# Attention scores on four quarters of the array, with v loaded by pairs of heads and rows of two weights permuted

## The chip, the cores and the metric

The kernel runs on one core of one Trainium2 chip. The metric is the device time of one execution in microseconds (us); the figure quoted for a kernel is the median of its runs. Engines are named as in the profile: PE is the matrix engine (PEld its weight loads), DVE the vector engine, ACT the scalar engine, POOL the GpSimd engine, SP the engine whose queue issues most of the DMAs ("SPq").

## The reference

The inputs q, k and v have 4 batches, 8 heads, 576 positions and 64 features per head. The positions are cut into 9 chunks of 64, and attention stays within a chunk. The result, laid out as 2304 tokens of 512 features, goes through a bilinear MLP and then through an MLP with a rational activation:

```python
scores = scale * np.matmul(q_c, k_c.transpose(0, 1, 2, 4, 3))
scores = scores - np.max(scores, axis=-1, keepdims=True)
attn = np.exp(scores)
attn = attn / (np.sum(attn, axis=-1, keepdims=True) + 1e-09)
x = np.matmul(attn, v_c)                  # then 2304 tokens x 512 features
x = ((x @ w_a) * (x @ w_b)) @ w_out       # 512 -> 1536 -> 512
...                                       # second MLP, 512 -> 2048 -> 512
```

A chunk's scores for one head are a product of 64x64 by 64x64, all in float32. Weights come as float64.

## The kernel before, in words

Activations are kept transposed: features on the 128 partitions, tokens along the free axis. The array has 128 rows (the contraction) and 128 columns (the output partitions); a product of 64 by 64 occupies one of its four quarters, given by a group of 64 rows and a group of 64 columns.

**Attention** works in 18 units of 128 tokens, which are two chunks c = 0, 1. `a_load` (line 270) brings q, k and v of a unit on SP, one DMA each of 256 KB with 128 partitions (chunk and position) by 8 heads by 64 features. A unit whose two chunks lie in different batches (units 4 and 13) takes two DMAs of 64 partitions each instead. `a_transpose` (294) turns k and q by PE into (h2, d) on the partitions, where a pair of heads hp holds heads 2 hp and 2 hp + 1 and h2 says which. `a_scores` (305) makes 16 products. Product (hp, c, h2) reads rows h2 of qT and kT and writes partitions h2 of one PSUM tile:

```python
r, cols = (slice(n * CH, (n + 1) * CH) for n in (h2, c))
nc.tensor.matmul(ps[r, 2 * hp + c, :], qT[r, hp, cols], kT[r, hp, cols], ...)
```

So the row group and the column group of a product are both h2, and two of the four quarters are used. A float32 product is two MATMUL instructions, so a unit has 32 of them at line 313. DVE then takes the maximum over the keys (317, one instruction of 128x512), subtracts it (319) and ACT takes the exponential (320). `a_soft` (323) normalizes, `a_ptrans` (331) transposes the probabilities by PE, and `a_pv` (342) multiplies with v: 16 products, row group c, column group h2, in the order (row, column) = (0,0), (0,1), (1,0), (1,1), with one PSUM tile for each c. ACT copies the two tiles out as the rounded part of x (358), DVE makes the low part (362). The transposes of units 4 and up, the scores of all, and the products with v of units 4 and up take their PSUM from `ps_at`, a pool of two buffers.

**Order of work.** The program is written out by hand in issue order for each engine. The four units of the first block of tokens come at the start in the order of the list FIRST (line 70: k and q transposes, S scores, E softmax, P transpose, V product with v, L low part, w one weight tile rounded, d products that nothing reads), their loads and the first four weight tiles in that of LOADS (73). Then come the loads of the two small operands ca and cb (545, 546), then, as tiles are rounded, more weight tiles, eight ahead, and after the last item of FIRST the loads of unit 4 (570). All of these DMAs are issued by SP, one after the other. The 14 later units are spread over the first MLP of the block of tokens before theirs: `a_pieces` (366) gives each piece a due time in twelfths of the unit's share, and `fill` (582) calls it between the halves of a step. There the pieces stand in PE's stream between long runs of products of the two MLPs. The load of v of the next unit is issued right behind the product with v (373), that of k and q behind the transpose of q.

**Weights.** `w_fetch` (137) loads one tile of 512 KB by one DMA. For w_a and w_b (and w_in of the second MLP) a tile is 128 columns of the matrix, with 128 partitions by 4 groups of rows by 1 KB (122). The 128 rows that share a group kk are contracted at once by `ab_half` (411). ACT and DVE round the tile (162 to 216) and w_out tiles come as 128 rows of 4 KB.

Of the kernel before, what the change touches and what calls it, by code (L numbers as in the profile page):

```python
# [20 lines left out]
def chunk_attention_two_mlps(  # L21
# [14 lines left out]
    """Chunked attention, a bilinear MLP, and an MLP with a rational activation.  # L36

    Activations are kept transposed (features on partitions, tokens along the free axis), so
    every product contracts over partitions without a transpose between layers. A float32
    operand x of the four large products is held as hi + lo, both float32r with 12 significant  # L40
    bits: hi is x rounded, lo = x - hi is exact. Then x @ w = hi @ w_hi + lo @ w_hi + hi @ w_lo
    in three passes of the tensor engine; lo @ w_lo lies below float32's rounding.

    The weights come as the bits of float64 (int64 of the same shape) and are rounded to float32
    here, from the two words H and L of an element. H, read as float32 and times 2**-112, has
    float32's exponent of the element in the bits 27 to 23 and the upper 20 bits of its fraction in
    the bits 22 to 3 of the word that three places further left are the element's without its sign
    and the last three bits; round(L * 2**-29) is added for those, and the sign is that of H in a
    float16 too small for any other bit. (An element below 2**-119 becomes one of that size or 0.)
    """  # L50
# [14 lines left out]
    # ln is taken of Q * 2**-LSH, which keeps it inside the table's range for any finite Q.  # L65
    LSH = 60
    # Order of the attention of the first block: transposes of k and q, scores, softmax, transpose of
    # its result, product with v and the low part of that; w: a weight tile is rounded; d: the tensor
    # engine is kept busy.
# [4 lines left out]
    # Tiles of weights that are loaded ahead of those rounded.  # L74
    AHEAD = 8
    # The attention of a block is spread over this part of the 3 * F1 places of the block before.
    SPAN = 33
    AN = 1280
    # Blocks of tokens of the first MLP. The first one is large: its steps wait for the weights.
# [3 lines left out]
    # Blocks of tokens of the second MLP.  # L83
# [27 lines left out]
    # ---------------------------------------------------------------- weights  # L111
# [5 lines left out]
    for nm, w, n, col in (("a", w_a, F1, True), ("b", w_b, F1, True), ("o", w_out, F1, False),  # L117
                          ("i2", w_in2, F2, True), ("o2", w_out2, F2, False)):
        bits = w.bitcast(I32)
        for i in range(n):  # L120
            if col:
                w_src[nm, i] = bits[:, 2 * i * P:2 * (i + 1) * P].rearrange("(k p) f -> p k f", p=P)
            else:
                w_src[nm, i] = bits[i * P:(i + 1) * P, :]
# [12 lines left out]
    def w_fetch():  # L137
        key = order[n_cv[0]]
        at = n_cv[0] + AHEAD
        n_cv[0] += 1  # L140
        if at < len(order1):
            t = p_w.tile([P, DM, 2], I32, name="w_raw", tag=f"w{at}")
        else:
            t = p_st.tile([P, DM, 2], I32, name="w_raw", tag="w_raw")
        dst = t.rearrange("p f t -> p (f t)")
        src = w_src[key]
        if len(src.shape) == 3:
            dst = dst.rearrange("p (k f) -> p k f", k=src.shape[1])
        nc.sync.dma_start(out=dst, in_=src)  # L149
        raws[key] = t  # L150
# [11 lines left out]
    def w_front(finish=lambda: None):  # L162
        """What ACT has to do with the next weight tile to be rounded, and the loads ahead of it."""
        while n_cv[0] < len(order) and n_cv[0] < n_cv[1] + (
            AHEAD if n_cv[0] + AHEAD < len(order1) else 3 if n_cv[0] < len(order1) else 2
        ):
            w_fetch()
        if n_cv[1] == len(order):
            held_w.append(finish)
            return  # L170
        t = raws.pop(order[n_cv[1]])
        hw = t[:, :, 1]
        lw = t.rearrange("p f t -> p (f t)").bitcast(U16).rearrange("p (f t) -> p f t", t=4)[:, :, 1]
        # Room for the terms: where the parts of the tile will be, or one more of p_st.
        if order[n_cv[1]] in w2_d:
            t = p_st.tile([P, 2, DM], I32, name="w_cz", tag="w_raw")
            c, z = t[:, 0], t[:, 1]
        else:
            c, z = w_tile(order[n_cv[1]], I32)
        zz = z.bitcast(F16).rearrange("p (f t) -> p f t", t=2)  # L180
        nc.scalar.activation(c.bitcast(F32), hw.bitcast(F32), AF.Copy, scale=2.0 ** -112)
        nc.scalar.activation(zz[:, :, 1], hw.bitcast(F32), AF.Copy, scale=2.0 ** -112)
        front_w.append((c, z))

        def rest():
            finish()
            nc.scalar.activation(zz[:, :, 0].bitcast(U16), lw, AF.Copy, scale=2.0 ** -13)

        held_w.append(rest)
# [5 lines left out]
    def w_next(n, hold=False):  # L195
        """Round the next n weight tiles; those of the first MLP stay on chip, those of the second
        go back to memory as float32. What is left of the last one comes with the next call."""
# [33 lines left out]
    def w2_next():  # L231
        """Split the next weight tile of the second MLP."""
# [16 lines left out]
    # -------------------------------------------------------------- attention  # L249
# [7 lines left out]
    # q, k and v of the units of the first block, where the last weights will be.  # L257
# [4 lines left out]
    # A ring of tokens for x and then for y.  # L262
# [7 lines left out]
    def a_load(u, *names):  # L270
        """[(c, s), h, d] for the chunks c = 0, 1 of unit u"""
        (b0, c0), (b1, c1) = divmod(2 * u, NCH), divmod(2 * u + 1, NCH)
        for nm, src in (("k", k), ("q", q), ("v", v)):
# [9 lines left out]
            if b0 == b1:  # L283
# [10 lines left out]
    def a_transpose(u, nm):  # L294
        """[(c, s), hp, (h2, d)] -> [(h2, d), hp, (c, s)]"""
# [9 lines left out]
    def a_scores(u):  # L305
        """[(h2, q), (hp, c), key], less its maximum over the keys; its exponential"""
        qT, kT = un.pop(("qT", u)), un.pop(("kT", u))
        ps = ps_at.tile([P, H, CH], F32, name="at", tag="at")
        for hp in range(HP):
            for c in range(2):  # L310
                for h2 in range(2):
                    r, cols = (slice(n * CH, (n + 1) * CH) for n in (h2, c))
                    nc.tensor.matmul(  # L313
                        ps[r, 2 * hp + c, :], qT[r, hp, cols], kT[r, hp, cols], start=True, stop=True
                    )
        m = p_e.tile([P, H], F32, name="m", tag="m")
        nc.vector.tensor_reduce(m, ps, AX.X, ALU.max)
        e = (p_t0 if u < U0 else p_t).tile([P, H, CH], F32, name="e", tag="T")
        nc.vector.tensor_tensor(e, ps, m.unsqueeze(2).to_broadcast([P, H, CH]), ALU.subtract)
        nc.scalar.activation(e, e, AF.Exp, scale=SCALE)  # L320
        un["e", u] = e
# [9 lines left out]
    def a_ptrans(u):  # L331
        """[(h2, q), hp, (c, key)] -> [(c, key), hp, (h2, q)]"""
# [9 lines left out]
    def a_pv(u):  # L342
        """x^T: [(h2, d), hp, (c, q)], a bank for each c: c is the row group of its products."""
        pT, vv = un.pop(("pT", u)), raw.pop(("v", u))
        ps = []
        for c in range(2):
            pool, tag = (ps_acc, "acc") if u < U0 else (ps_at, "at")
            ps.append(pool.tile([P, HP, CH], F32, name="at", tag=tag))
        for hp in range(HP):
            for c in range(2):  # L350
                for h2 in range(2):
                    r, cols = (slice(n * CH, (n + 1) * CH) for n in (c, h2))
                    nc.tensor.matmul(  # L353
                        ps[c][cols, hp, :], vv[r, 2 * hp + h2, :], pT[r, hp, cols], start=True, stop=True
                    )
        out = [[t[:, :, x_at(u * P + c * CH, CH)] for t in (x_hi, x_lo)] for c in range(2)]
        for c, (hi, lo) in enumerate(out):
            nc.scalar.copy(hi, ps[c])  # L358

        def low():  # L360
            for c, (hi, lo) in enumerate(out):
                nc.vector.tensor_tensor(lo, ps[c], hi.bitcast(F32), ALU.subtract)  # L362
# [3 lines left out]
    def a_pieces(u):  # L366
        """With the twelfth of the time at which each is due."""
# [8 lines left out]
    # -------------------------------------------------------- constants a, b  # L376
# [4 lines left out]
    # ---------------------------------------------------------------- phase 1  # L381
# [45 lines left out]
    # ---------------------------------------------------------------- phase 2  # L427
# [9 lines left out]
    def y_split(j, kk):  # L437
        """For even blocks where x was, for odd ones where the last weights of the first MLP were."""
# [19 lines left out]
    def g_front(j, i):  # L458
        """Denominator less 1 + 1e-6 and numerator less a0, both from h."""
# [13 lines left out]
    def g_back(u, t):  # L473
        """Their quotient: 1 / Q as exp(-ln Q) and one Newton step."""
# [59 lines left out]
    def warm(n):  # L534
        """Products that nothing reads: the tensor engine's clock falls while it idles."""
# [43 lines left out]
    for j in range(NB):  # L579
# [11 lines left out]
        for i in range(F1):  # L591
            def w_more(part):
                """At an even pace, three tiles ahead of those in use."""
# [82 lines left out]
```

## Time and profile before

| | |
|---|---|
| median of 3 runs | 939.78 us (937.49 to 939.79) |
| span of the profiled execution | 934.7 us |
| median less span (what lies around the span) | 5.1 us |
| PE busy | 917.6 us, 98% of the span |
| DVE, ACT busy | 613.2 us (66%), 588.4 us (63%) |
| DMA queue of SP | 91776 packets, 67.65 MB |

The span runs from the first to the last instruction of the profiled execution. Its own total time is not listed apart from the runs, so the difference to the median stands for what lies around the span. Busy time of PE is modelled from start times and lengths; where one matmul overlaps the next, the chain of waits tells better what a group costs. "Idle before" in a row is the time in which the engine stood still just before those instructions.

### The profile page before, as it was taken

What the parts mean: (1) busy time and instruction counts of PE and PEld (TensorE: products, weight loads), DVE (VectorE), ACT (ScalarE), POOL (GpSimd) and SP (SyncE); (2) the same over time, 40 slices, a digit from 0 to 9 for tenths busy, and PEclk for the clock granted to TensorE, in tenths of its full rate; (3) what the DMA queues carried; (4) which work ended last, traced back from release to release, by engine and by line L of the source; (5) the groups of instructions that cost most, each with busy time, mean ns of one, the idle gap of its engine ahead of it and who ended that gap; (6) DMA issues with size and microseconds to landing.
All of it is one profiled execution on the core that took longest, in us unless ns stands there. A gap on an engine that the chain in (4) does not pass through costs nothing.

```text
span 934.7 us, 14740 instructions
## 1 busy us (share of the span) xinstructions
PE 917.6 (98%) x5828; PEld 829.9 (89%) x5828; DVE 613.2 (66%) x1074; ACT 588.4 (63%) x1068; POOL 18.1 (2%) x38
## 2 busy tenths in 40 slices
PE   6799999999999999999999999999999999999998
PEld 6688889999999999999999999888888888888997
DVE  3787863334443344344255579999879988998886
ACT  5899983225445445444244488877677767767775
POOL 0000000000000000000000000000000000000000
PEclk8999999999999999999999999999999999999999
DMA  9983242214445453443154300020011002000100
GB/s 226 278 274 115 87 149 80 58 40 137 132 133 158 133 162 124 124 147 102 53 155 148 109 34 1 1 80 1 1 40 52 1 1 79 1 0 1 46 1 35
DMA packets 97863, 81.72 MB, mean 87 GB/s; under 512 B 59648, under 2 KB 83712, under 8 KB 97792
## 3 DMA queue, kind: packets, MB, share of 16 engines
q1 hardware_dynamic: 91776, 67.65, 25.2%
q0 software_dynamic: 2560, 8.39, 2.4%
q10 hardware_dynamic: 3456, 4.72, 1.4%
q8 instruction: 46, 0.75, 0.4%
q14 instruction: 25, 0.20, 0.1%
HBM read 62.92 MB, written 17.83 MB: 86 GB/s over the span
## 4 chain that ended last, share of the span: by engine, by line
PE 95%; SPq 3%; DMA 1%; issue 0%; ACT 0%
PE acc L242 13%; PE acc L243 12%; PE acc L244 12%; PE ab L242 11%; PE ab L244 11%; PE ab L243 11%; PE h L242 7%; PE h L244 7%; PE h L243 7%; PE at L313 2%; SPq L291 2%; PE at L300 1%; SPq L149 1%; DMA k<-in_k_dram 1%; PE at L353 1%; PE at L337 1%
## 5 line engine op out<-in xcount | busy, mean ns | idle before, releaser
L242 PE MATMUL ab<-x_hi,w 128*128 128x384 f32 (+2 forms) x576 | 196.8, 342 | 0.7 <-ACT x_hi L358 0.7
L243 PE MATMUL ab<-x_lo,w 128*128 128x384 f32 (+2 forms) x576 | 193.0, 335 | 0.0
L244 PE MATMUL ab<-x_hi,w 128*128 128x384 f32 (+2 forms) x576 | 193.0, 335 | 0.0
L242 PEld LDWEIGHTS ab<-x_hi,w 128*128 128x128 f32 x576 | 108.5, 188 | 5.8 <-ACT x_hi L358 0.9
L244 PE MATMUL acc<-w,g_lo 128*128 128x512 f32 x288 | 112.6, 391 | 0.0
L243 PE MATMUL acc<-w,g_hi 128*128 128x512 f32 x288 | 112.6, 391 | 0.0
L242 PE MATMUL acc<-w,g_hi 128*128 128x512 f32 x288 | 112.1, 389 | 0.0
L243 PEld LDWEIGHTS ab<-x_lo,w 128*128 128x128 f32 x576 | 108.6, 189 | 3.9 <-DVE x_lo L362 0.3
L244 PEld LDWEIGHTS ab<-x_hi,w 128*128 128x128 f32 x576 | 108.4, 188 | 3.8
L465 ACT ACTIVATE a_ring<-h 128x512 f32<-128x512 f32 (+1 forms) x80 | 44.2, 552 | 86.4 <-PE h L244 86.4
L242 PE MATMUL acc<-g_hi,w 128*128 128x384 f32 (+2 forms) x288 | 98.4, 342 | 0.0
L244 PE MATMUL acc<-g_hi,w 128*128 128x384 f32 (+2 forms) x288 | 96.4, 335 | 0.0
L243 PE MATMUL acc<-g_lo,w 128*128 128x384 f32 (+2 forms) x288 | 96.4, 335 | 0.0
L425 DVE TENSOR_TENSOR g_lo<-a_ring,g_hi 128x384 fp32r<-128x384 f32 (+2 forms) x72 | 40.1, 557 | 80.3 <-ACT g_hi L422 80.3
L419 DVE TENSOR_TENSOR a_ring<-ab,a_ring 128x384 f32<-128x384 f32 (+2 forms) x72 | 39.9, 554 | 78.0 <-PE ab L244 77.8
L608 ACT COPY a_ring<-ab 128x384 f32<-128x384 f32 (+2 forms) x72 | 34.4, 478 | 73.0 <-PE ab L244 72.5
L468 DVE SCALAR_TENSOR_TENSOR u<-u,cb_t,a_ring 128x512 f32<-128x512 f32 (+1 forms) x80 | 55.6, 696 | 28.8 <-ACT u L466 28.1
L244 PE MATMUL h<-x_hi,w 128*128 128x384 f32 (+1 forms) x192 | 68.0, 354 | 0.0
L242 PE MATMUL h<-x_hi,w 128*128 128x384 f32 (+1 forms) x192 | 68.0, 354 | 0.0
L243 PE MATMUL h<-x_lo,w 128*128 128x384 f32 (+1 forms) x192 | 67.9, 353 | 0.0
L244 PEld LDWEIGHTS acc<-w,g_lo 128*128 128x128 f32 x288 | 54.0, 188 | 11.3
L422 ACT CAST g_hi<-a_ring 128x384 fp32r<-128x384 f32 (+2 forms) x72 | 36.2, 503 | 43.7 <-DVE a_ring L419 43.7
(85 smaller groups left out, 1828.4 us busy)
## 6 DMA issues: line engine op xcount, KB each, us to landing
w_raw<-in_moe_w_out_dram SPq DMA_DIRECT2D x28, 512.0 KB, 4.7
w_raw<-in_moe_w_in_dram SPq DMA_DIRECT2D x16, 512.0 KB, 4.2
w_raw<-in_moe_w_a_dram SPq DMA_DIRECT2D x12, 512.0 KB, 6.6
w_raw<-in_moe_w_b_dram SPq DMA_DIRECT2D x12, 512.0 KB, 6.8
out_dram<-o SPq DMA_DIRECT2D x18, 256.0 KB, 2.5
w_i<-w_x POOLq DMA_DIRECT2D x16, 256.0 KB, 2.3
w_o<-w_x POOLq DMA_DIRECT2D x16, 256.0 KB, 2.3
w_raw<-w_i SPq DMA_DIRECT2D x16, 256.0 KB, 2.7
```

What stands on the lines that cost most here:

```text
L149: nc.sync.dma_start(out=dst, in_=src)
L242: nc.tensor.matmul(ps, wh, xh, start=first, stop=False)
L243: nc.tensor.matmul(ps, wh, xl, start=False, stop=False)
L244: nc.tensor.matmul(ps, wl, xh, start=False, stop=last)
L291: nc.sync.dma_start(out=dst, in_=s.rearrange("h s d -> s h d"))
L313: nc.tensor.matmul(ps[r, 2 * hp + c, :], qT[r, hp, cols], kT[r, hp, cols], start=True, stop=True)
L419: nc.vector.tensor_tensor(a_s, ps_b, a_s, ALU.mult)
L422: nc.scalar.copy(hi, a_s)
L425: return lambda: nc.vector.tensor_tensor(lo, a_s, hi.bitcast(F32), ALU.subtract)
L465: nc.scalar.activation(ah, ps, AF.Abs)
L468: nc.vector.scalar_tensor_tensor(u, u, cb_t[:, 0:1], ah, ALU.add, ALU.mult)
L608: nc.scalar.copy(a_s, ps_a)
```

## The change

Scores: the product (hp, c, h2) now writes the partitions of chunk c, into a PSUM tile of its own for each h2. Its row group is h2 and its column group is c, so all four quarters are used, in the order (row, column) = (0,0), (1,0), (0,1), (1,1). Maximum and subtraction are done for each of the two tiles (four DVE instructions of 128x256 in place of two of 128x512). The probabilities then lie with (chunk, query) on partitions, and their transpose has (h2, key) there. So v is loaded with h2 and key on the partitions: four DMAs for each unit, of 64 partitions by 4 heads. The product with v has h2 as its row group and b as its column group (head 4b + 2a + h2), in the same order of quarters as the scores. This leaves the features of x in another order, which the rows of w_a and w_b follow: a tile of theirs is loaded by two DMAs of 64 partitions each. Comments and docstrings are also blanked.

```diff
@@ weights
                 w_src[nm, i] = bits[:, 2 * i * P:2 * (i + 1) * P].rearrange("(k p) f -> p k f", p=P)
+                if nm in "ab":
+                    w_src[nm, i] = bits[:, 2 * i * P:2 * (i + 1) * P].rearrange(
+                        "(b k d) f -> b d k f", b=2, d=D
+                    )
@@ w_fetch
-        nc.sync.dma_start(out=dst, in_=src)
+        if len(src.shape) == 4:
+            for b in range(2):
+                nc.sync.dma_start(out=dst[b * D:(b + 1) * D], in_=src[b])
+        else:
+            nc.sync.dma_start(out=dst, in_=src)
@@ a_load
-            if b0 == b1:
+            if nm == "v":
+                t = t.rearrange("p (c a) d -> p c a d", c=2)
+                parts = [
+                    (t[h2 * CH:(h2 + 1) * CH, c], src[bb, h2::2, cc * CH:(cc + 1) * CH, :])
+                    for c, (bb, cc) in enumerate(((b0, c0), (b1, c1)))
+                    for h2 in range(2)
+                ]
+            elif b0 == b1:
@@ a_scores
-        ps = ps_at.tile([P, H, CH], F32, name="at", tag="at")
+        ps = [ps_at.tile([P, HP, CH], F32, name="at", tag="at") for _ in range(2)]
...
-                    nc.tensor.matmul(
-                        ps[r, 2 * hp + c, :], qT[r, hp, cols], kT[r, hp, cols], start=True, stop=True
-                    )
+                    nc.tensor.matmul(ps[h2][cols, hp, :], qT[r, hp, cols], kT[r, hp, cols], start=True, stop=True)
-        nc.vector.tensor_reduce(m, ps, AX.X, ALU.max)
-        nc.vector.tensor_tensor(e, ps, m.unsqueeze(2).to_broadcast([P, H, CH]), ALU.subtract)
+        for h2 in range(2):
+            nc.vector.tensor_reduce(m[:, h2], ps[h2], AX.X, ALU.max)
+        for h2 in range(2):
+            nc.vector.tensor_tensor(
+                e[:, :, h2], ps[h2], m[:, h2].unsqueeze(2).to_broadcast([P, HP, CH]), ALU.subtract
+            )
@@ a_pv
-            ps.append(pool.tile([P, HP, CH], F32, name="at", tag=tag))
+            ps.append(pool.tile([P, 2, P], F32, name="at", tag=tag))
...
-                    nc.tensor.matmul(
-                        ps[c][cols, hp, :], vv[r, 2 * hp + h2, :], pT[r, hp, cols], start=True, stop=True
-                    )
+                        nc.tensor.matmul(
+                            ps[h2][cols, a, q], vv[r, c, 2 * b + a, :], pT[r, 2 * b + a, q], start=True, stop=True
+                        )
```

In the new `a_pv` the loops run over a, c, b, h2, outermost first, with `r, cols, q` for h2, b, c. The copies of x out of PSUM and its low part stay two of 128x256 for each unit.

## Rows read from the trace of the kernel before

**Rows 1.** Span and busy time of the engines, from the page's head and part 1.

```profile
span 934.7 us, 14740 instructions
...
PE 917.6 (98%) x5828; PEld 829.9 (89%) x5828; DVE 613.2 (66%) x1074; ACT 588.4 (63%) x1068; POOL 18.1 (2%) x38
```

**Rows 2.** Windows, core 0: stretch and length in us, busy us per engine, PEclk, DMA share, GB/s.

```profile
50.00:60.00 10.00, 10.00 (x64) 8.30 (x61) 8.92 (x17) 10.00 (x18) 0.00 (x0) 1.00 1.07 367
...
140.00:450.00 310.00, 310.00 (x2594) 301.90 (x2592) 124.03 (x249) 137.23 (x269) 16.74 (x31) 1.00 0.39 118
```

**Rows 3.** Chain of waits in order of time: start us, us on the chain, what.

```profile
146.68 1.08 PE at L313 x32
...
147.76 0.32 PE ab L242
...
158.53 0.62 PE at L353 x32
...
159.16 0.32 PE ab L242
...
337.87 0.62 PE at L353 x32
...
433.12 1.08 PE at L313 x32
```

**Rows 4.** Line 353 on PE's queue: count, then min/median/max ns.

```profile
L353 PEldq EVENT_SEMAPHORE  x19: 51/51/318, 28.5 to 446.1; - x19
```

**Rows 5.** Instruction groups by line and shape: count, busy us, mean ns, idle before.

```profile
L362 DVE TENSOR_TENSOR x_lo<-at,x_hi 128x256 fp32r<-128x256 f32 x36 | 13.4, 417 | 11.6 <-ACT x_hi L358 11.5
...
L317 DVE TENSOR_REDUCE m<-at 128x8 f32<-128x512 f32 x18 | 12.4, 691 | 38.7 <-PE at L313 38.5
```

**Rows 6.** DMA issues on SP, lines 291 and 149: count, min/median/max ns.

```profile
L291 SPq DMA_DIRECT2D v<-in_v_dram x16: 367/368/2899, 35.8 to 423.8; - x16
...
L291 SPq DMA_DIRECT2D kqv<-in_k_dram x4: 432/1118/2517, 0.7 to 13.5; - x4
...
L149 SPq DMA_DIRECT2D w_raw<-in_moe_w_a_dram x12: 367/466/1465, 2.9 to 114.7; - x12
```

**Rows 7.** The same for line 291, 312 to 314 us only: two pieces of half height.

```profile
L291 SPq DMA_DIRECT2D v<-in_v_dram x2: 607/617/627, 312.2 to 312.9; - x2
```

**Rows 8.** Timeline of SP, first 31 us: start us, us, line, issue.

```profile
13.45 2.52 SPq L291 DMA_DIRECT2D kqv<-in_k_dram  x1
16.02 0.96 SPq L291 DMA_DIRECT2D kqv<-in_v_dram  x1
17.02 1.15 SPq L149 DMA_DIRECT2D w_raw<-in_moe_w_a_dram  x1
18.21 0.56 SPq L291 DMA_DIRECT2D kqv<-in_v_dram  x1
18.82 1.04 SPq L545 DMA_DIRECT2D ca_t<-in_moe_a_dram  x1
19.90 1.52 SPq L546 DMA_DIRECT2D cb_t<-in_moe_b_dram  x1
21.46 0.44 SPq L149 DMA_DIRECT2D w_raw<-in_moe_w_b_dram  x1
...
29.38 1.74 SPq L291 DMA_DIRECT2D k<-in_k_dram  x2
```

**Rows 9.** Windows of the opening: busy us per engine, PEclk, DMA share, GB/s.

```profile
23.00:24.00 1.00, 0.70 (x7) 0.46 (x5) 0.95 (x3) 0.78 (x2) 0.00 (x0) 1.00 0.76 51
24.00:25.00 1.00, 0.00 (x0) 0.00 (x0) 0.95 (x3) 0.87 (x3) 0.00 (x0) 1.00 0.46 84
```

**Rows 10.** Chain of waits around the first load of unit 4.

```profile
30.15 9.96 DMA k<-in_k_dram
40.24 0.63 PE at L300 x4
```

**Rows 11.** Waits: who for whom, us in total, times, longest.

```profile
PE at L300 <- DMA k<-in_k_dram: 1.1, 1, 1.1
```

More of the change, by code (lines that the diff above doesn't have):

```diff
@@ L146, in w_fetch @@
         src = w_src[key]
-        if len(src.shape) == 3:
-            dst = dst.rearrange("p (k f) -> p k f", k=src.shape[1])
-        nc.sync.dma_start(out=dst, in_=src)
+        if len(src.shape) > 2:
+            dst = dst.rearrange("p (k f) -> p k f", k=src.shape[-2])
+        if len(src.shape) == 4:
[3 more added lines that the diff above has]
+            nc.sync.dma_start(out=dst, in_=src)
         raws[key] = t
@@ L312, in a_scores @@
                     r, cols = (slice(n * CH, (n + 1) * CH) for n in (h2, c))
[L313 to L319 removed]
+                    nc.tensor.matmul(ps[h2][cols, hp, :], qT[r, hp, cols], kT[r, hp, cols], start=True, stop=True)
+        m = p_e.tile([P, 2, HP], F32, name="m", tag="m")
+        e = (p_t0 if u < U0 else p_t).tile([P, HP, 2, CH], F32, name="e", tag="T")
+        for h2 in range(2):
[4 more added lines that the diff above has]
+            )
         nc.scalar.activation(e, e, AF.Exp, scale=SCALE)
[L321 removed]
+        un["e", u] = e.rearrange("p a b d -> p (a b) d")
     def a_soft(u):
@@ L345, in a_pv @@
         ps = []
-        for c in range(2):
+        for h2 in range(2):
             pool, tag = (ps_acc, "acc") if u < U0 else (ps_at, "at")
-            ps.append(pool.tile([P, HP, CH], F32, name="at", tag=tag))
-        for hp in range(HP):
+            ps.append(pool.tile([P, 2, P], F32, name="at", tag=tag))
+        for a in range(2):
             for c in range(2):
-                for h2 in range(2):
-                    r, cols = (slice(n * CH, (n + 1) * CH) for n in (c, h2))
-                    nc.tensor.matmul(
-                        ps[c][cols, hp, :], vv[r, 2 * hp + h2, :], pT[r, hp, cols], start=True, stop=True
-                    )
-        out = [[t[:, :, x_at(u * P + c * CH, CH)] for t in (x_hi, x_lo)] for c in range(2)]
-        for c, (hi, lo) in enumerate(out):
-            nc.scalar.copy(hi, ps[c])
+                for b in range(2):
+                    for h2 in range(2):
+                        r, cols, q = (slice(n * CH, (n + 1) * CH) for n in (h2, b, c))
+                        nc.tensor.matmul(
+                            ps[h2][cols, a, q], vv[r, c, 2 * b + a, :], pT[r, 2 * b + a, q], start=True, stop=True
+                        )
+        out = [
+            [t.rearrange("p (a b) n -> p b a n", b=2)[:, h2, :, x_at(u * P, P)] for t in (x_hi, x_lo)]
+            for h2 in range(2)
+        ]
+        for h2, (hi, lo) in enumerate(out):
+            nc.scalar.copy(hi, ps[h2])
         def low():
-            for c, (hi, lo) in enumerate(out):
-                nc.vector.tensor_tensor(lo, ps[c], hi.bitcast(F32), ALU.subtract)
+            for h2, (hi, lo) in enumerate(out):
+                nc.vector.tensor_tensor(lo, ps[h2], hi.bitcast(F32), ALU.subtract)
         un["lo", u] = low
```

## The prediction

> **What bounds the kernel now.** I read the page's first part, then windows, then the chain of waits. PE is busy for 98% of the span [rows 1], and from 140 to 450 us, where twelve of the 18 units of attention lie, it has no idle time at all while DVE is busy for 40% and ACT for 44% [rows 2]. In the chain every group of the attention on PE stands as a piece of its own between products of the MLPs [rows 3]. So behind the opening each microsecond that the attention's matmuls save shortens the kernel, as long as nothing else comes late. The opening is another stage: PE waits there for loads, for DVE and for ACT, and the last wait before its long unbroken run is for k of unit 4: the load is on the chain for 9.96 us, PE starts its transposes at 40.24 us [rows 10] after standing still for 1.1 us [rows 11]. What happens before that is worth nothing unless this load moves.
>
> **The scores.** The two kinds of products of the attention have the same count of instructions (32 for each unit) and the same shape, 64x64 by 64x64 in float32. The scores, on two quarters, take 1.08 us of the chain, the products with v, on four quarters, 0.62 us [rows 3]. What follows each of them on the chain takes the same 0.32 us, so nothing of the difference is given back there. That is 33.6 ns against 19.4 ns for an instruction with its weight load. After the change the scores use four quarters, so I take the price of the products with v: 1.08 - 0.62 = 0.46 us for a unit. The rows nearest below and above are 0.62 and 1.08 itself (no gain); the value below 0.62 is a rival, further down. Units 0 to 3 lie in the opening and count for nothing. Units 4 to 17 give 14 x 0.46 = 6.4 us. The unit at 433.12 us shows the same 1.08 as the one at 146.68 [rows 3], so one price holds for all. Two of the 14 units lie in the first block's MLP, where ACT is busy for 10.00 of 10.00 us between 50 and 60 [rows 2]; should PE run into ACT there, 2 x 0.46 = 0.9 us go, which leaves 5.5.
>
> [...]
>
> **The products with v** keep their count and their four quarters; only the order of the quarters changes. I take no change here. They now wait for four loads of v instead of one or two. A further wait is an instruction of 51 ns on PE's queue [rows 4], at most 3 x 0.051 x 14 = 2.1 us. The product of unit 13, whose v came in two DMAs, took 0.62 like the others [rows 3]: PE's queue handles the waits while the array works on what is ahead, so I take 0.
>
> **DVE.** Maximum and subtraction become four instructions of 128x256. One of 512 elements takes 0.69 us, one of 256 read from PSUM 0.42 us [rows 5], so a unit costs DVE 2 x (0.84 - 0.69) = 0.30 us more, 5.4 us over all. The exponential and the softmax behind it start that much later, and PE asks for their result only some pieces of the schedule later, after long runs of MLP products; DVE has 60% of its time free there [rows 2]. I take 0. If that cover were gone it would be 14 x 0.30 = 4.2 us.
>
> **PSUM.** The scores now take both buffers of their pool. From unit 4 on, the second buffer is the one that the copy of qT has just left, and the scores need that copy as data anyway: 0. In the opening S1 and S2 stand side by side in the list, and S2 must now wait until DVE has subtracted for S1: up to 4 x 0.42 = 1.7 us of PE, with V0 behind it. Faster scores give back up to 0.46 us each there. Both fall before the wait for k of unit 4, which has 1.1 us to spare, so I take 0.
>
> **SP's queue** is where the change costs. A unit's v was one DMA and becomes four of half height; a tile of w_a or w_b becomes two. A load of full height in a quiet stretch takes SP 0.37 us to issue [rows 6], but pieces of half height took 0.62 us each [rows 7], although they carry half as much. I take 0.62 for every new piece; the lower end is half of the full price, 0.18. In the opening the least a load takes is 0.43 us, a weight tile's median is 0.47 [rows 6]. So a load of v costs SP 4 x 0.62 - 0.43 = 2.0 us more, a weight tile 2 x 0.62 - 0.47 = 0.8 us more. From unit 4 on this is hidden: v is issued right behind the unit's product with v and needed at the next unit's. Behind it in SP's queue stand weight tiles that are loaded ahead of need, and k and q, also a unit ahead.
>
> In the opening it isn't clear. Up to 15.97 us SP issues 10 loads of 256 KB and 3 weight tiles. At 0.43 and 0.47 us these would take 5.7 us of the 15.2 us since its first issue at 0.74 us; the other 9.5 us SP is held back because the DMA engines are full, as in the 2.52 us of one issue [rows 8]. Two loads of v and two split tiles add 5.6 us up to there, which fits. Then v of unit 1, the tile of w_a and v of unit 3 take 0.96, 1.15 and 0.56 us [rows 8] and will need 2.47, 1.23 and 2.47: 3.5 us more. The two small loads behind them, 1.04 and 1.52 us [rows 8], may hold up to 1.7 us of holding back that can make room. Next comes the tile of w_b at 21.46 us, and there the DMA engines are short of work already: from 23 to 25 us they move 51 and 84 GB/s, at a share of 0.76 and 0.46 [rows 9]. So what delays this issue delays everything behind it, k of unit 4 included, and PE with it. After it the queue fills again: k of unit 4 is issued at 29.38 us [rows 8] and lands some 10 us later [rows 10], so the five further tiles that are split (5 x 0.8 = 4 us) stay hidden. I take a delay of 2.0 us, between 3.5 - 1.7 and 3.5; the ends are 0 and 10.5 us (all that is added before that tile: 4 x 2.0 + 3 x 0.8).
>
> **Sum.** - 6.4 + 2.0 = - 4.4 us. The profiled execution has a span of 934.7 us [rows 1], 5.1 us under the median of the runs, 939.8; what lies around the span doesn't change, so the span becomes 930.3 and the median 935.4 us. With gain 5.5 to 6.4 and delay 0 to 3.5, the forecast's own range is 933.4 to 937.8. A difference under 0.3%, 2.8 us, can't be told from none here: faster means under 937.0, slower over 942.6.
>
> **Rivals.**
> 1. *Another order of quarters is better still.* Before, a quarter that computes scores takes an instruction every 2 x 33.6 = 67 ns, and neighbours alternate between the row groups. A quarter that multiplies with v takes one every 4 x 19.4 = 78 ns, and there pairs of neighbours share a row group. After, neighbours always alternate. If a quarter's own pace of 67 ns is then reached, 32 instructions take 0.54 us: the scores gain 0.54 and the products with v 0.08, together 14 x 0.62 = 8.7 us, and the time is 933.1 us. [...] Chance 0.12.
> 2. *The end on the other side: SP's pieces.* If nothing is held back where I count on it, the whole 10.5 us before the w_b tile push k of unit 4 back, and the time is 939.8 - 6.4 + 10.5 = 943.9 us. The place is the same wait at 40 us; it decides from a delay of 6.4 us on. For it: 0.62 us for a half piece, and the gap in the DMA at 23 us. Against it: 9.5 us of holding back, and PE's 1.1 us of waiting is all that this load costs now. [...] Chance 0.17, half of it beyond 942.6 or close to it.
> 3. *The change doesn't do what it says.* In the new order neighbours share a column group, hence the same PSUM partitions, in two banks; before, neither kind of product did that. If they then run one behind the other, scores stay at 1.08 and only the delay is left: 941.8 us; if the products with v fall to 1.08 as well, 948.2. Against it: four quarters at work already share PSUM partitions by pairs. Chance 0.13.
>
> **Numbers.** The forecast has 0.58. Faster: 0.50 of the forecast and rival 1, 0.62. Within 0.3%: the rest of the forecast, half of rival 2 and most of rival 3, 0.27. Slower: 0.11. The range runs from 932.0 (rival 1 with a small delay) to 942.5 (rival 3, and the nearer half of rival 2).
>
> **What would show it.** Right: pieces of 32 instructions at the scores' line at about 0.62 us on the chain, the products with v unchanged, no new idle time before the scores from unit 4 on, the transposes of k of unit 4 starting near 42 us with a wait of about 3 us. Wrong: scores still near 1.08 or products with v longer; a start of those transposes later than 46 us; PE waiting for softmax results or for v behind 140 us; SP issues of half pieces far from 0.62 us.

## The result, and the profile after

The changed kernel takes 945.67 us, the median of 4 runs (945.24 to 946.14), against 938.63 us for the kernel before in 4 runs beside it (937.25 to 939.79). The ratio is 1.008 with a 95% interval of [1.0057, 1.0102]: it is slower by some 7.5 us (0.8%), where 4.4 us of gain were forecast, and the time lies above the range (932.0 to 942.5). The profiled executions differ by 944.4 - 934.7 = 9.7 us in span, and the reading below goes by these. They differ by more than the medians do because the profiled execution of the kernel before was a fast one: time and span of one run lie only 1.7 to 1.8 us apart (946.14 and 944.4 here), so most of the 5.1 us that were put down to what lies around the span is that.

The page's head and part 1, to be read against [rows 1]:

```profile
span 944.4 us, 14909 instructions
...
PE 913.4 (97%) x5828; PEld 823.6 (87%) x5828; DVE 613.9 (65%) x1110; ACT 588.5 (62%) x1068; POOL 18.1 (2%) x38
```

PE does the same 5828 matmuls in 4.2 us less of busy time, yet the span is 9.7 us longer. So PE has less work and stands still for longer. Chain of waits of the changed kernel, in order of time (start us, us on the chain, what); lines 316, 330 and 374 are the transposes, scores and products with v that stood at 300, 313 and 353:

```profile
31.60 11.46 DMA w_raw<-in_moe_w_b_dram
43.08 10.89 DMA k<-in_k_dram
54.11 1.09 PE at L316 x4
...
162.12 0.62 PE at L330 x32
...
173.53 0.62 PE at L374 x32
...
443.58 0.62 PE at L330 x32
```

The scores now take 0.62 us where they took 1.08 [rows 3], in the unit at 162 us and in the last one alike, and the products with v still take 0.62. But the transposes of k of unit 4 start at 54.11 us where they started at 40.24 [rows 10]. The waits and PE's timeline say why (who for whom, us in total, times, longest; then start, us, what, and in brackets the idle time before it):

```profile
PE at L316 <- DMA k<-in_k_dram: 12.8, 1, 12.8
ACT kT L318 <- PE at L316: 25.6, 8, 13.3
```

```profile
54.11 1.09 PE L316 MATMUL at<-ident,k 128*128 128x128 f32 x4 [12.82 <-DMA k<-in_k_dram]
...
58.90 0.60 PE L316 MATMUL at<-ident,q 128*128 128x128 f32 x4
```

and q of unit 4 in the kernel before:

```profile
43.47 0.60 PE L300 MATMUL at<-ident,q 128*128 128x128 f32 x4
```

A wait of 1.1 us [rows 11] has become one of 12.8 us, and ACT stands idle for 13.3 us behind the copy of the same transposes, with the rounding of weights queued behind that copy. What the stall then costs can be followed at three places of the two traces, and at their ends:

| start of | before | after | difference |
|---|---|---|---|
| k of unit 4 on PE | 40.24 | 54.11 | + 13.9 |
| q of unit 4 on PE | 43.47 | 58.90 | + 15.4 |
| scores of unit 6 | 146.68 | 162.12 | + 15.4 |
| end of the span | 934.7 | 944.4 | + 9.7 |

The second step, from k to q, is 1.6 us, over the same twelve products of the MLP. It is the clock. Windows of the changed kernel (stretch and length in us, busy us of PE, PEld, DVE, ACT, POOL with counts, PEclk, DMA share, GB/s):

```profile
44.00:46.00 2.00, 0.00 (x0) 0.00 (x0) 0.00 (x0) 0.00 (x0) 0.00 (x0) 0.50 1.17 216
...
54.00:56.00 2.00, 1.89 (x7) 1.73 (x8) 0.00 (x0) 0.77 (x2) 0.00 (x0) 0.50 0.44 98
56.00:58.00 2.00, 2.00 (x8) 1.57 (x7) 0.86 (x2) 2.00 (x4) 0.00 (x0) 0.64 0.88 214
```

While PE stands still, the granted clock falls to 0.50 (from 0.95 at 42 to 44 us), and it is still there from 54 to 56 us and, with a mean of 0.64, for a part of the next window, when PE has work again; the transposes of k take 1.09 us there and took 0.63 [rows 10] at a clock of 1.00. From q of unit 4 to the scores of unit 6 nothing is won or lost (103.2 us in either kernel), although the scores of units 4 and 5 lie between: the 0.9 us that the prediction took off for its lower bound didn't come. The chain of the changed kernel says what sets the pace there. Behind the transposes of q it passes to ACT, which rounds weights, and stays on ACT and DVE until PE takes it over at 149.88 us:

```profile
60.02 0.66 ACT w L190
...
149.23 0.61 DVE a_ring L443
149.88 0.50 PE ab L251
```

From unit 6 on, twelve units give back 15.4 - 9.7 = 5.7 us, and 12 x 0.46 would be 5.5. Nothing else came late there, since PE is busy for 309.87 of 310 us:

```profile
140.00:450.00 310.00, 309.87 (x2602) 298.94 (x2601) 130.40 (x283) 146.47 (x286) 16.87 (x31) 1.00 0.41 121
```

The last part is SP's queue, from its timeline (start us, us, line, issue, count), against [rows 8]:

```profile
7.14 6.13 SPq L307 DMA_DIRECT2D kqv<-in_v_dram  x4
...
21.35 2.18 SPq L156 DMA_DIRECT2D w_raw<-in_moe_w_a_dram  x2
23.58 2.59 SPq L307 DMA_DIRECT2D kqv<-in_v_dram  x4
26.21 0.60 SPq L569 DMA_DIRECT2D ca_t<-in_moe_a_dram  x1
26.86 0.43 SPq L570 DMA_DIRECT2D cb_t<-in_moe_b_dram  x1
27.34 1.27 SPq L156 DMA_DIRECT2D w_raw<-in_moe_w_b_dram  x2
...
42.19 1.49 SPq L307 DMA_DIRECT2D k<-in_k_dram  x2
```

The tile of w_b is issued at 27.34 us where it was issued at 21.46: 5.9 us late (2.0 were forecast). From there to the transposes of k it takes 54.11 - 27.34 = 26.8 us, where it took 18.8: another 8.0 us (none were forecast). The two make the 13.9 us. The price of one issue was right, counts and min/median/max ns by [rows 7]:

```profile
L156 SPq DMA_DIRECT2D w_raw<-in_moe_w_a_dram x24: 596/611/1518, 2.9 to 130.8; - x24
...
L307 SPq DMA_DIRECT2D v<-in_v_dram x56: 596/612/2746, 49.9 to 436.2; - x56
```

SP's price per piece was forecast, so it alone doesn't explain a delay of this size. The page's part 3 shows a first trace of something else: as many bytes on the queue as before, but they hold the DMA engines for longer. Queue, packets, MB and share of 16 engines, first of the changed kernel, then of the kernel before:

```profile
q1 hardware_dynamic: 92992, 67.65, 28.2%
```

```profile
q1 hardware_dynamic: 91776, 67.65, 25.2%
```

### The profile page after: what moved, and what is told of

It reads as the page before. It is cut to its first block, busy times and chain, and to the rows that moved or that the text cites. A ratio compares the mean times of both kernels' runs of the same rounds, so it can differ in the third digit from the quotient of the medians.

```text
span 944.4 us, 14909 instructions
## 1 busy us (share of the span) xinstructions
PE 913.4 (97%) x5828; PEld 823.6 (87%) x5828; DVE 613.9 (65%) x1110; ACT 588.5 (62%) x1068; POOL 18.1 (2%) x38
## 3 DMA queue, kind: packets, MB, share of 16 engines
q1 hardware_dynamic: 92992, 67.65, 28.2%
## 4 chain that ended last, share of the span: by engine, by line
PE 84%; ACT 6%; SPq 3%; DMA 2%; DVE 2%; issue 1%; DVEq 0%; ACTq 0%
PE acc L251 11%; PE acc L252 11%; PE acc L253 11%; PE ab L251 9%; PE ab L252 9%; PE ab L253 8%; PE h L251 7%; PE h L253 7%; PE h L252 7%; SPq L307 2%; ACT w L168 1%; PE at L316 1%; DMA w_raw<-in_moe_w_b_dram 1%; ACT w L191 1%; DMA k<-in_k_dram 1%
## 5 line engine op out<-in xcount | busy, mean ns | idle before, releaser
L251 PEld LDWEIGHTS acc<-w,g_hi 128*128 128x128 f32 x288 | 54.1, 188 | 10.6 <-ACT a_ring L428 0.2
```

The costliest lines, as they stand in the source:

```text
L251: nc.tensor.matmul(ps, wh, xh, start=first, stop=False)
```

## The experiments

Two questions: is anything of the loss in the scores themselves, and what of the loads makes k late, SP's price for more pieces or the way the DMA engines move pieces of 64 partitions? The medians of the kernel before lie between 936.6 and 939.4 us from one set of runs to the next, so kernels are compared by their ratio to it.

### The scores without the loads

The loads stay as they were. The products are put on the four quarters the other way round: the row group is h2 as before, the column group is the lower bit g of the pair of heads, and the product with v reads the probabilities from where they then lie.

```diff
+        ps = [ps_at.tile([P, HP, CH], F32, name="at", tag="at") for _ in range(2)]
+        for b in range(2):
+            for c in range(2):
+                for g in range(2):
+                    for h2 in range(2):
...
+                        hp = 2 * b + g
+                        nc.tensor.matmul(
+                            ps[h2][rows, 2 * b + c, :], qT[r, hp, cols], kT[r, hp, cols], start=True, stop=True
+                        )
@@ a_pv
-   ps[c][cols, hp, :], vv[r, 2 * hp + h2, :], pT[r, hp, cols], ...
+   ps[c][cols, hp, :], vv[r, 2 * hp + h2, :], pT[r, 2 * h2 + hp // 2, (hp % 2) * CH:(hp % 2 + 1) * CH], ...
```

> The kernel before with one part of the change alone, in another layout: scores on all four quarters (row group h2, column group the lower bit of the pair hp, a PSUM tile for each h2, four DVE instructions of 128x256), with v, w_a and w_b loaded as before. Theory A (the matmuls gain what was forecast and all of the loss comes from the split loads in the opening) and theory B (the same, but by the number of DMAs): scores 0.62 us a unit on the chain, transposes of k of unit 4 at 40 to 41 us, time 5.5 to 6.4 us under the kernel before, about 932.2 to 933.1 us beside 938.6. Theory C (the scores taking both PSUM buffers and the longer DVE work cost the time, in the opening and in the first MLP block): no gain or a loss, 938 us or more, and transposes of k of unit 4 clearly later than 40 us.

931.06 us, ratio 0.9937 [0.9915, 0.9959]: faster than the kernel before and the changed one. Chain, and PE's timeline at k of unit 4:

```profile
145.50 0.62 PE at L315 x32
...
426.96 0.62 PE at L315 x32
```

```profile
38.83 0.63 PE L300 MATMUL at<-ident,k 128*128 128x128 f32 x4 [0.48 <-DMA k<-in_k_dram]
```

The gain is 0.0063 x 938 = 5.9 us (2.1 either way), within the 5.5 to 6.4 us of the prediction. That it lies above 5.5 is partly luck. In the profiled executions the gain is 934.7 - 928.0 = 6.7 us, of which 1.2 stand already at the scores of unit 6 (145.50 against 146.68) and come from a k of unit 4 that was there 1.4 us earlier; the other 5.5 are twelve units. The scores of units 4 and 5 gave nothing here either. The four DVE instructions, the two PSUM tiles and the new order of quarters, all of which this kernel has too, cost nothing that the time shows: theory C falls, which leaves the loads.

### The loads without the scores

The kernel before, with v in four pieces of 64 partitions and tiles of w_a and w_b in two, nothing else changed:

```diff
+            if nm == "v":
+                parts = [
+                    (t[c * CH:(c + 1) * CH, HP * a:HP * (a + 1)], src[bb, HP * a:HP * (a + 1), cc * CH:(cc + 1) * CH, :])
+                    for c, (bb, cc) in enumerate(((b0, c0), (b1, c1)))
+                    for a in range(2)
+                ]
@@ w_fetch
+        if key[0] in "ab":
+            for b in range(2):
+                nc.sync.dma_start(out=dst[b * D:(b + 1) * D], in_=src[b * D:(b + 1) * D])
...
```

> The kernel before with the loads alone split as in the change: v in four pieces of 64 partitions by 4 heads, each tile of w_a and w_b in two pieces of 64 partitions; all data land where they did before and the products are those of before. Theories A and B: the whole loss of the opening and nothing of the gain, transposes of k of unit 4 near 54 us, time 12 to 15 us over the kernel before, about 951 to 954 us. Theory C: 938 to 941 us, transposes near 40 to 42 us.

949.93 us, ratio 1.0128 [1.0105, 1.0151], a little under what theories A and B forecast. Timeline of PE:

```profile
52.70 1.09 PE L310 MATMUL at<-ident,k 128*128 128x128 f32 x4 [11.79 <-DMA k<-in_k_dram]
```

The loads alone bring the late k, and its transposes take the same 1.09 us as in the changed kernel at 0.50 (here the granted clock was 0.57 on average from 42 to 50 us, while PE stood still). With the gain of the first experiment taken off, 1.0128 - 0.0063 = 1.0065, and the changed kernel shows 1.008: within the intervals the two edits add up.

### As many pieces, each over all partitions

A piece spans 128 partitions and holds as many bytes as in the second experiment (v: two heads; weights: two of the four groups of rows). The count of DMAs is the same, except that v of units 4 and 13 stays in two DMAs as in the kernel before. The edit of the weights, against the second experiment:

```diff
-                nc.sync.dma_start(out=dst[b * D:(b + 1) * D], in_=src[b * D:(b + 1) * D])
+                nc.sync.dma_start(out=dst[:, 2 * b:2 * (b + 1)], in_=src[:, 2 * b:2 * (b + 1)])
...
```

> As the run with the split loads, with as many pieces of as many bytes, but each piece keeps all 128 partitions: v in four pieces of 2 heads (as before for the two units that cross a batch), each tile of w_a and w_b in two pieces of 2 groups of rows. Theory A (height: a piece on 64 partitions costs SP more and moves at about 210 GB/s in place of about 350): pieces cost SP 0.37 to 0.45 us, transposes of k of unit 4 at 40 to 44 us, time 938 to 943 us. Theory B (number: each DMA costs SP its price, and SP may have only a few in flight): transposes near 54 us and 950 to 954 us, as with the half pieces.

940.33 us, ratio 1.003 [1.0017, 1.0043]. PE's timeline; issues of w_a; a window:

```profile
43.70 1.09 PE L309 MATMUL at<-ident,k 128*128 128x128 f32 x4 [5.47 <-DMA k<-in_k_dram]
```

```profile
L151 SPq DMA_DIRECT2D w_raw<-in_moe_w_a_dram x24: 367/458/965, 2.7 to 120.4; - x24
```

```profile
30.00:36.00 6.00, 4.03 (x44) 2.93 (x43) 5.17 (x13) 4.59 (x11) 0.00 (x0) 0.83 1.08 369
```

More pieces by themselves cost k 3.5 us (43.70 against 40.24) and the kernel 0.3%; pieces of half the partitions cost 12.5 us and 1.3%. Issue is cheaper here (0.46 us) and the engines move 369 GB/s. Both accounts, issue and movement, still stand: the next pair parts them.

### Half the partitions: one half of them, or every second one

Only the tiles of w_a and w_b are split, v is loaded as before. First by halves 0 to 63 and 64 to 127 (the w_fetch lines of the second experiment alone):

> The kernel before with the tiles of w_a and w_b alone in two pieces of 64 partitions, 0 to 63 and 64 to 127. Theory A (height): the eight tiles that are ahead of k of unit 4 hold 4.2 MB; at 215 in place of some 350 GB/s they take 7.5 us longer, so transposes of k of unit 4 at 45 to 49 us and 943 to 947 us. Theory B (the v pieces with their price on SP are the main cost): transposes near 41 to 43 us and 938 to 941 us.

Then by even and odd partitions, with the same number of partitions, bytes and packets for each DMA (against the run with halves):

```diff
-                nc.sync.dma_start(out=dst[b * D:(b + 1) * D], in_=src[b * D:(b + 1) * D])
+                nc.sync.dma_start(out=dst[b::2], in_=src[b::2])
```

> The same split of w_a and w_b into two pieces of 64 partitions, but one piece has the even and the other the odd partitions, so that each reaches all over the 128. [...] Theory N (the number of 64 partitions, or the number of DMAs, makes it slow): as the run with the halves 0 to 63 and 64 to 127, at about 215 GB/s, 943 to 947 us. The price of a piece on SP tells by itself whether that hangs on the number (0.61 us) or on the place (0.47 us).

By halves: 946.55 us, ratio 1.0103 [1.0076, 1.0129]. Even and odd: 937.76 us, ratio 1.0 [0.9984, 1.0016]. The kernel with halves: SP's issue of the tile of w_b and PE's timeline, issues of w_a, two windows behind the tile of w_b, the queue's share on the page:

```profile
23.41 1.26 SPq L151 DMA_DIRECT2D w_raw<-in_moe_w_b_dram  x2
```

```profile
48.34 1.09 PE L304 MATMUL at<-ident,k 128*128 128x128 f32 x4 [9.81 <-DMA k<-in_k_dram]
```

```profile
L151 SPq DMA_DIRECT2D w_raw<-in_moe_w_a_dram x24: 595/602/1437, 2.7 to 124.7; - x24
```

```profile
32.00:34.00 2.00, 0.85 (x16) 0.61 (x20) 2.00 (x7) 1.12 (x3) 0.00 (x0) 1.00 1.15 200
34.00:36.00 2.00, 1.25 (x34) 0.80 (x29) 1.87 (x5) 1.46 (x4) 0.00 (x0) 1.00 1.13 227
```

```profile
q1 hardware_dynamic: 92160, 67.65, 28.4%
```

The kernel with even and odd partitions, the same views:

```profile
21.21 1.27 SPq L151 DMA_DIRECT2D w_raw<-in_moe_w_b_dram  x2
```

```profile
40.14 1.09 PE L304 MATMUL at<-ident,k 128*128 128x128 f32 x4 [3.31 <-DMA k<-in_k_dram]
```

```profile
L151 SPq DMA_DIRECT2D w_raw<-in_moe_w_a_dram x24: 602/612/1468, 2.6 to 118.0; - x24
```

```profile
26.00:28.00 2.00, 1.94 (x27) 1.68 (x22) 1.62 (x3) 1.09 (x3) 0.00 (x0) 1.00 1.06 390
28.00:30.00 2.00, 2.00 (x68) 1.69 (x66) 1.86 (x6) 1.44 (x4) 0.00 (x0) 1.00 1.09 353
```

```profile
q1 hardware_dynamic: 92160, 67.65, 25.0%
```

SP pays the same 0.60 to 0.61 us for both kinds of piece, where a piece of as many bytes over 128 partitions took 0.46 in the third experiment: in these runs that price hangs on the count of partitions, not on which they are, and for the weights it costs nothing (937.76 us, ratio 1.0). What differs is the movement: 200 and 227 GB/s against 390 and 353 at a DMA share over 1 in either kernel (1.15 and 1.13 against 1.06 and 1.09), so the engines are full in both, but with pieces of one half they carry (200 + 227) / (390 + 353), under six tenths as much. The tile of w_b is issued 2.0 us late with halves and 0.2 us early with even and odd partitions; from there to the transposes of k it is 6.1 us longer with halves and 0.1 us with the others. So the movement of the weight tiles makes k 8.1 us late, and theory N falls: with as many partitions and as many DMAs, even and odd pieces are not slow. The profiled execution with even and odd partitions is 2.1 us longer in span than that of the kernel before (936.8 and 934.7): its k comes on time, but PE has stood still for 3.3 us and begins at a granted clock of 0.50 (from 40 to 46 us). The medians of the two kernels show no difference.

What the two runs leave open is that their pieces also read different rows of the matrix, 64 neighbouring ones or every second one. Against that rival speaks the changed kernel, whose halves take their rows in another order than those of the second experiment and hold the engines for the same 28.2%. Why pieces of one half move more slowly, no run shows; what the runs show are the rates.

### Only v in pieces

> The kernel before with the loads of v alone in four pieces of 64 partitions by 4 heads. SP's queue gets 4 x 2.0 us longer before the w_b tile that was issued at 21.46 us. Theory A: some of it is taken up by holding back, that tile is issued 2 to 5 us later and k of unit 4 follows, transposes at 42 to 45 us, 939 to 943 us. Theory B (pieces of v carry most of the loss): transposes at 48 us or later and 945 us or more.

The a_load lines of the second experiment alone: 943.13 us, ratio 1.0067 [1.0041, 1.0092], just beyond the end of theory A and short of theory B. PE's timeline, SP's timeline, two windows and the queue's share on the page:

```profile
45.20 1.09 PE L306 MATMUL at<-ident,k 128*128 128x128 f32 x4 [7.32 <-DMA k<-in_k_dram]
```

```profile
25.27 0.43 SPq L149 DMA_DIRECT2D w_raw<-in_moe_w_b_dram  x1
```

```profile
26.00:28.00 2.00, 2.00 (x42) 1.81 (x41) 1.51 (x3) 1.69 (x3) 0.00 (x0) 1.00 0.05 6
...
34.00:36.00 2.00, 1.40 (x5) 0.96 (x6) 1.40 (x4) 2.00 (x5) 0.00 (x0) 1.00 1.06 377
```

```profile
q1 hardware_dynamic: 92608, 67.65, 25.1%
```

Here most of the delay lies ahead of the tile of w_b (issued 3.8 us late); behind it the unsplit tiles move at 377 GB/s.

This delay is of another kind than that of the weights. Pieces of v, whose rows are 256 bytes, hold the engines no longer than whole loads did: 25.1% of the span against 25.2%, where the halves of the weights brought 28.4%. Instead the engines run out of work: at 26 to 28 us, behind the pieces of v, their share is 0.05. A piece holds 64 KB and costs SP 0.61 us (the changed kernel's median), so by an estimate from these two numbers SP can hand out no more than about 107 GB/s while it issues v. In the third experiment, where no piece of the first block has half height and each costs SP less, k was still 3.5 us late. So the loss by v looks like SP's price for more pieces; no run changed that price alone.

How late the tile of w_b was issued, and how much longer it then took to the transposes of k, against the kernel before:

| | tile of w_b | from there to k | together |
|---|---|---|---|
| weights by halves | 2.0 | 6.1 | 8.1 |
| weights even and odd | - 0.2 | 0.1 | - 0.1 |
| v in pieces | 3.8 | 1.2 | 5.0 |
| changed kernel | 5.9 | 8.0 | 13.9 |

The weights and v alone add up to 13.1 us, against 12.5 in the second experiment and 13.9 in the changed kernel. The times do so only just within the intervals: 0.67% + 1.03% against 1.28%.

### Scores on two quarters with a PSUM tile each

Whether the speed-up comes from the four quarters or from the two separate tiles: the kernel before with a tile for each h2, still on two quarters. DVE works on 64 partitions at a time for it, so its time is not to be compared.

```diff
-   ps[r, 2 * hp + c, :], qT[r, hp, cols], kT[r, hp, cols], ...
+   ps[h2][r, 2 * hp + c, :], qT[r, hp, cols], kT[r, hp, cols], ...
```

> The kernel before with the scores still on two quarters (row group and column group h2), but a PSUM tile of its own for each h2, as in the change; DVE works on 64 partitions by 512 elements, two times each. Theory Q (the number of quarters sets the pace): scores stay at 1.08 us a unit on the chain. Theory K (two row groups writing into one PSUM bank held the scores up, and separate banks free them): scores fall towards 0.62 us without the other two quarters.

One execution, 950.4 us. Its chain:

```profile
196.94 1.08 PE at L314 x32
...
221.76 1.08 PE at L314 x32
```

The price stays at 1.08 us: theory Q holds. The four quarters make the scores faster (0.62 us); separate tiles alone don't.

### The second halves of the weights on another queue

The changed kernel, with half of the pieces of w_a and w_b issued by POOL.

```diff
-                nc.sync.dma_start(out=dst[b * D:(b + 1) * D], in_=src[b])
+                (nc.sync, nc.gpsimd)[b].dma_start(out=dst[b * D:(b + 1) * D], in_=src[b])
```

> The changed kernel, with the second half (partitions 64 to 127) of every tile of w_a and w_b issued by POOL in place of SP, so that the two halves travel at the same time on two queues. [...] Theory M (64 partitions a DMA move slowly in any case, or the permuted rows of the source do): still about 215 GB/s, transposes at 50 us or later, 943 us or more.

962.92 us, ratio 1.0271 [1.0248, 1.0294], far slower than the changed kernel. PE's timeline:

```profile
31.50 1.09 PE L316 MATMUL at<-ident,kqv 128*128 128x128 f32 x4 [18.14 <-DMA kqv<-in_k_dram]
```

POOL has nothing else to do at the start and issued 15 of its halves from 1.5 to 19.0 us. Eight of them went out before SP came to the load of k of unit 1 at 6.4 us, and that load landed at 31.4 us. The order of the loads had changed, not only their queue, so the run says nothing on the question it was made for, and theory M is neither better nor worse for it.

### k and q of unit 4 ahead of the weights

If the one wait for k carries the loss, then loading k and q of unit 4 before the weight tiles takes it away while the slow movement stays. The changed kernel, with only this:

```diff
         a_load(int(item[1]), item[0])
+    a_load(U0, "k", "q")
...
-    a_load(U0, "k", "q", "v")
+    a_load(U0, "v")
```

> The changed kernel with k and q of unit 4 loaded earlier, right behind the loads of the first block, ahead of eight weight tiles in SP's queue. Theory V (the slow stream itself bounds the opening, whatever stands last in it): the transposes of k no longer wait, but weights come late by as much: ACT and PE wait for weight tiles instead, and most of the loss stays, 941 to 946 us. Theory K (only the place of k of unit 4 behind the weights makes the loss, since PE and ACT stand still behind it): 932 to 938 us, near the gain that the scores alone bring.

932.19 us, ratio 0.9945 [0.9927, 0.9963]. A window:

```profile
44.00:48.00 4.00, 4.00 (x19) 3.29 (x19) 2.86 (x6) 4.00 (x8) 0.00 (x0) 1.00 1.15 208
```

The DMA engines still move only 208 GB/s at a share over 1, and PE is busy all the time: the weights have that much room. No wait for k is left. The control is the kernel before with the same move:

> Control: the kernel before with k and q of unit 4 loaded behind the loads of the first block, as in the last run of the changed kernel, and nothing else. If moving these loads is worth something only where the stream before them is slow: the 1.1 us of waiting go at most, 936.5 to 938.5 us. If it is what made the changed kernel fast with them, apart from the scores: some 4 to 6 us under the kernel before, 932 to 934 us.

935.45 us, ratio 0.9969 [0.9953, 0.9985]. So the move is worth 0.3% (2.9 us) where k was hardly late, and 1.35% (12.7 us) in the changed kernel. The control lies between its two forecasts. The 9.8 us between the two moves are what the late k cost the changed kernel beyond what the move is worth anyway: theory K holds and V falls, but for what the last run leaves open.

### The scores without the loads, and the move

> Scores on four quarters with natural loads, and k and q of unit 4 loaded early. Its wait for that k was 0.5 us, so 930 to 931.5 us, not to be told from the version without the move. If the opening of that version was still bounded there, up to 2 us less, 929 us.

929.59 us, ratio 0.9899 [0.9882, 0.9917], the fastest of all: 0.7% beyond the control, 0.63% without the move. Within the intervals the gain of the scores and that of the move add up. Against the changed kernel with the move (0.9945) it is better by 0.46%, some 4 us, while the profiled executions of the two differ by only 0.5 us of span (928.4 and 928.9). Whether slow movement costs something more, beyond the wait for k, stays open.

## Why the prediction was wrong

**The scores: right.** 1.08 us became 0.62 in every unit behind the opening, and twelve units behind 140 us gave 5.7 us of span (12 x 0.46 = 5.5). The lower bound of 5.5 us was the right one: the scores of units 4 and 5 gave nothing, because ACT sets the pace in the first block, as the prediction had allowed for. The stall isn't the reason, since they gave nothing in the first experiment either, where ACT had no such stall.

**Products with v, DVE, PSUM: right.** The products stayed at 0.62 us in the new order, which is where rivals 1 and 3 fall. Rival 1 compared 67 ns with 78 ns for a quarter. These contain a longer step at the start of each unit (100 and 87 ns); behind it the records show a quarter starting an instruction every 58 ns in either kind of product, with two quarters at work or four. The maximum took 418 ns for 128x256 as in [rows 5] for such a shape. The first experiment has all these costs but the loads, and it gained what the term for the scores said.

**SP's price: right.** 0.61 us for a half piece.

**The delay: this step failed.** The prediction says "I take a delay of 2.0 us" for the tile of w_b and, of the five split tiles from there on, that they "stay hidden". Measured were 5.9 us up to the tile of w_b and 8.0 us from there to k, 13.9 in place of 2.0.

The greater part is movement, a term that the prediction doesn't have. It counted what SP pays to issue pieces and took for granted that the engines then move them as fast as before. Weight tiles by halves of the partitions moved at 200 and 227 GB/s, where even and odd pieces moved at 390 and 353, so the stretch behind the tile of w_b, in which the prediction let the full queue hide the pieces, was the very stretch that grew: here a full queue hid the issue but not the movement. With weights alone this made 8.1 us of delay, 2.0 up to the tile and 6.1 behind it; even and odd pieces, with the same price on SP, made none.

The smaller part is the holding back (in the kernel before, issues of up to 2.86 us at a DMA share of 1.04 to 1.34 from 2 to 16 us), a term that the prediction sized too large. It let two loads of v and two split tiles, 5.6 us, vanish in it ("which fits"), but v of unit 1, issued next, was already 2.3 us late (18.34 against 16.02). The three loads behind that took 5.1 us more, where 3.5 were counted, and the two small loads gave back 1.5. Some of this is movement again; v in pieces alone made 3.8 us of it, by SP's price as far as the runs show.

Nor did the range cover the whole: its upper end of 10.5 us was again a sum of issues.

**Rival 2** named the place, the wait for k of unit 4, and its side, and lay near the time (943.9 forecast, 945.67 measured). That is partly luck: it put all of its 10.5 us down to issues ahead of the tile of w_b, where 5.9 were measured, and the other 8.0 came behind it from a cause that it doesn't name. It had a chance of 0.17.

**What nobody priced:** the clock. After 12.8 us of standing still PE began at a granted clock of 0.50 and lost another 1.6 us.

Sum in spans: + 13.9 (k late) + 1.6 (clock) - 5.5 (twelve units at 0.46 us) = + 10.0, measured + 9.7.

## What to carry to other kernels

What a split load costs isn't only its issue: here weight tiles by halves of the partitions, in rows of 1 KB, moved at 200 and 227 GB/s against 390 and 353 for even and odd pieces at the same 0.60 to 0.61 us an issue, while pieces of v, in rows of 256 bytes, held the engines no longer than before (25.1% against 25.2%) and cost by their number, as far as the runs show. If a layout needs pieces of 64 partitions, look first for one that spreads them over all 128 partitions (here even and odd ones, 937.76 us against 946.55). A change of layout for one engine's sake is priced at every load that follows from it: here the same four quarters were to be had by another choice of heads, with no load changed. And in an opening that waits for loads, look at what stands in the queue ahead of the one load that the whole kernel waits for, before pricing anything else.

## What the hardware showed unexpectedly

SP needed longer to issue a DMA of 64 partitions (0.60 to 0.61 us, by halves or by every second one) than one of 128 partitions with the same bytes (0.46 us), which the third to fifth experiments show side by side. Scores on two quarters kept their 1.08 us whether the two halves share a PSUM tile or not. And PE's granted clock in the changed kernel did not rise at once when work came back at 54.11 us: it was 0.50 from 54 to 56 us and 0.64 on average from 56 to 58 us. It had been at 0.50 once before, from 38 to 40 us, with PE busy in all of these 2 us; from 34 to 36 us, at full clock, PE had been busy for 1.26 of 2 us.
